# A fused attention and maxout kernel: one low part, one sum, one minimum and two weight loads change place

## The chip, the cores and the metric

The kernel runs on one core of one Trainium2 chip. Its engines are TensorE (PE in the profile; PEld is its weight load), VectorE (DVE), ScalarE (ACT), GpSimd (POOL) and SyncE (SP), which here issues all the transfers. The metric is the time on the device in microseconds, as the median of several runs.

## The reference

Two steps, all in fp32. First, an attention through 32 inducing points: for each of 4 batches of 12,544 tokens with 128 channels, the inducing points attend over the tokens and give 32 states `h`, and then each token attends over these 32 states. Second, each token of the result goes through a maxout layer.

```python
def mab(q, kv):
    s = scale * (q @ kv.transpose(0, 2, 1))
    s = s - s.max(-1, keepdims=True)
    a = np.exp(s)
    a /= a.sum(-1, keepdims=True) + 1e-09
    return a @ kv
h = mab(I, x)
x = mab(x, h)                                       # B 4, N 12544, m 32, C 128
h = np.maximum(np.maximum(x @ w1, x @ w2), x @ w3)  # 128 by 768 each
out = h @ w_out                                     # 768 by 128
```

The weights of the maxout layer arrive as 64-bit numbers and are turned into fp32 on the chip.

## The kernel before

**Tiling.** The tokens of a batch are 98 tiles of 128, in seven groups: group 0 has 2 tiles, the others 16. For the second step a group of 16 tiles is four chunks of 512 tokens (the small group is one chunk of 256), so a batch has 25 chunks, and 768 hidden columns are six blocks of 128. One chunk with one block is a *slot*; there are 600.

**The products of a slot.** Since the maximum of three is max(x·w1 − x·w2, x·w3 − x·w2, 0) + x·w2, and x is the softmax's weights times the 32 states, the states are first multiplied by the weights (`us`, in a high and a low part), and each slot takes them by the weights `pT` of a chunk (again high and low parts, stacked on 128 partitions). A slot has these pieces, in `advance` (a step `s` handles the slots around `s`) and `stage2`:

- PE: `pu` (L663) of slot s+1, then `pv` (L669) of slot s, each into one of two banks;
- ScalarE: `ru = relu(pu)` (L678), then `hi`, the high part of `h` of the slot before (L685);
- VectorE: `h = max(pv, ru)` (L696);
- GpSimd, or for listed slots VectorE: `lo = h - hi` (L693 and L699). `LOWVEC = (23, 0, 15, 18)`, and `LOWLAST` in the last batch, list the slots of a group of 24 whose low part VectorE takes; it is then issued one step later, behind the next `h`;
- PE, six slots later (`LAG`): three products into the chunk's sum, `hi` by the high part of `w_out` (L719), `hi` by its low part (L720), `lo` by the high part (L721); once for a chunk L718 adds the part x·w2·w_out.

`h` has five buffers, `hi` and `lo` ten by name, of which the tile framework's own choice leaves fewer. A step's next `pv` writes the bank that `h` two slots back must have read.

**What runs between.** While batch b goes through its slots, the attention of batch b+1 is done group by group: products (L282), the greatest score and its spread to all quadrants (`attend_max` L292, `attend_column` L299, `attend_spread` L306), the running least value of its negative `mneg` (`attend_least`, L310 and L313), weights (L321), transposes (L335), sums over tokens (L345), and the addition to the running states, `hs` and `lst`, with the factor `al` (`attend_scale` L364, `attend_add` L382). The softmax of the second step runs one group ahead (`scores_steps`, L595 to L628). A plan by slot number says at which step each piece is issued; the engines run their instructions in that order.

**Before the main loop.** Batch 0's attention comes first, in `phase1_first`: loads of x by group, transposes on PE (L272), the same steps as above, and between them the conversion of the four weights in the steps of `WORK` ("2t" is step t, L171, of the weight of index 2, which is w1; index 3 is w3, 0 is w2, 1 is `w_out`). `LOADS` is the order in which SyncE issues the first loads: 0 to 6 are groups of x, 7 to 10 the weights w2, `w_out`, w1, w3. A group of 16 tiles has five buffers (`XB`), so that group 6 waits for the buffer of group 1.

Then `ORDER` is a list written out by hand, from about 42 to 54 us: `a` and `b` are the next step of the softmax of group 0 and of group 1; `0` to `3` a high part of `us` and `c` its low part; `m` another product for `us`; `p` and `q` the rows `pT` of chunk 0 and of chunk 1 (PE transposes and a copy for the first, L640 and L645; four DMAs for the second, L648); `d` two products of the identity that nobody reads (`keep_busy`, L393); `s` a step of `advance`; `S` the scores of group 2.

## Time and profile before

| | us |
|---|---|
| median of 3 runs | 832.28 |
| the runs | 831.1, 832.28, 832.58 |
| the profiled execution | 830.93 |
| its span, from the first to the last instruction | 828.8 |

| engine | busy, us | share of the span |
|---|---|---|
| TensorE products | 813.8 | 98% |
| TensorE weight loads | 632.9 | 76% |
| ScalarE | 743.5 | 90% |
| VectorE | 644.0 | 78% |
| GpSimd | 646.7 | 78% |

A share is an average over the span. What a stretch is bound by is read from the chain of waits and from the timeline, in which each row gives the start, the duration, the engine, the line with its operation, output and inputs, and in brackets how long the engine was idle before and whose work ended that. Products are pipelined on TensorE, so rows overlap, and the distance of two starts says more than a duration.

### The profile page before, as it was taken

How to read it: one execution, taken by the hardware profiler on the slowest of the kernel's cores; microseconds unless marked ns; L12 is line 12 of the kernel's file. 1: busy time of each engine (PE TensorE's matmuls, PEld its weight loads, DVE VectorE, ACT ScalarE, POOL GpSimd, SP SyncE). 2: the span in 40 equal slices, each digit the busy share in tenths (PEclk: the TensorE clock that was granted, in tenths of full speed). 3: DMA queues.
4: the chain of work that ended last, by engine and by line, in shares of the span. 5: the costliest groups of instructions: out<-in, count | busy, mean ns of one | idle time of the engine just before them, and what ended most of it. 6: DMA issues, size and time to landing. Idle time of an engine off the chain costs nothing.

```text
span 828.8 us, 14799 instructions
## 1 busy us (share of the span) xinstructions
PE 813.8 (98%) x4608; PEld 632.9 (76%) x4608; DVE 644.0 (78%) x1109; ACT 743.5 (90%) x1542; POOL 646.7 (78%) x517
## 2 busy tenths in 40 slices
PE   7989999999999999999999999999999999999998
PEld 5657778777787787777777777877778778778786
DVE  4878778878787688787787877877878778877864
ACT  6679889898898898898999989989889899999996
POOL 1368779778798697787887877877879888888887
PEclk9999999999999999999999999999999999999999
DMA  9744534433443445244334362441233222222221
GB/s 342 288 149 124 199 85 159 163 118 106 133 139 120 143 156 167 80 161 158 112 106 134 114 210 77 153 128 52 64 82 88 71 77 77 64 77 72 70 77 52
DMA packets 44062, 102.51 MB, mean 124 GB/s; under 512 B 9552, under 2 KB 13264, under 8 KB 38736
## 3 DMA queue, kind: packets, MB, share of 16 engines
q1 hardware_dynamic: 43984, 101.57, 37.8%
q8 instruction: 37, 0.61, 0.3%
q14 instruction: 41, 0.34, 0.1%
HBM read 48.12 MB, written 25.69 MB: 89 GB/s over the span
## 4 chain that ended last, share of the span: by engine, by line
PE 94%; DMA 2%; DVE 1%; SPq 1%; issue 1%; ACT 0%; DVEq 0%; ACTq 0%
PE acc L719 17%; PE acc L720 16%; PE acc L721 16%; PE pv L669 16%; PE pu L663 16%; PE aux L582 3%; PE acc L718 3%; PE acc L345 3%; PE aux L282 2%; DMA xg<-in_x_dram 2%; SPq L100 1%; DVE h L696 0%; PE acc L306 0%; PE acc L525 0%; SPq L120 0%
## 5 line engine op out<-in xcount | busy, mean ns | idle before, releaser
L693 POOL TENSOR_TENSOR lo<-h,hi 128x512 fp32r<-128x512 f32 (+1 forms) x498 | 631.5, 1296 | 141.5 <-ACT hi L685 102.9
L696 DVE TENSOR_TENSOR h<-pv,ru 128x512 f32<-128x512 f32 (+1 forms) x600 | 402.9, 675 | 152.3 <-PE pv L669 72.5
L678 ACT ACTIVATE ru<-pu 128x512 f32<-128x512 f32 (+1 forms) x600 | 375.4, 626 | 54.6 <-PE pu L663 50.6
L685 ACT CAST hi<-h 128x512 fp32r<-128x512 f32 (+1 forms) x600 | 386.5, 644 | 7.2 <-DVE h L696 6.8
L719 PE MATMUL acc<-hi,wo_hi 128*128 128x512 f32 (+1 forms) x600 | 237.2, 395 | 0.0
L669 PE MATMUL pv<-pT,us 128*128 128x512 f32 (+1 forms) x600 | 232.8, 388 | 3.8 <-DVE h L696 3.2
L663 PE MATMUL pu<-pT,us 128*128 128x512 f32 (+1 forms) x600 | 232.7, 388 | 0.3 <-DMA pT<-pl 0.3
L720 PE MATMUL acc<-hi,wo_lo 128*128 128x512 f32 (+1 forms) x600 | 231.6, 386 | 0.0
L721 PE MATMUL acc<-lo,wo_hi 128*128 128x512 f32 (+1 forms) x600 | 231.3, 385 | 0.0
L719 PEld LDWEIGHTS acc<-hi,wo_hi 128*128 128x128 f32 x600 | 112.7, 188 | 31.8 <-issue 10.4
L669 PEld LDWEIGHTS pv<-pT,us 128*128 128x128 f32 x600 | 112.6, 188 | 30.6 <-DVE h L696 8.8
L663 PEld LDWEIGHTS pu<-pT,us 128*128 128x128 f32 x600 | 112.6, 188 | 26.2 <-ACT ru L678 2.5
L721 PEld LDWEIGHTS acc<-lo,wo_hi 128*128 128x128 f32 x600 | 112.7, 188 | 23.1
L720 PEld LDWEIGHTS acc<-hi,wo_lo 128*128 128x128 f32 x600 | 112.8, 188 | 21.1
L699 DVE TENSOR_TENSOR lo<-h,hi 128x512 fp32r<-128x512 f32 x102 | 76.6, 751 | 6.4 <-PE acc L721 3.6
L726 ACT COPY o<-acc 128x512 f32<-128x512 f32 (+1 forms) x100 | 61.4, 614 | 3.0 <-PE acc L721 3.0
L718 PE MATMUL acc<-pT,us 128*128 128x512 f32 (+1 forms) x100 | 38.8, 388 | 0.0
L345 PEld LDWEIGHTS acc<-xg,aT 128*32 128x32 f32 x768 | 21.1, 110 | 11.4 <-issue 7.2
L282 PE MATMUL aux<-xT,iT 128*32 128x512 f32 x192 | 25.3, 598 | 1.6 <-ACT xT L274 1.6
L345 PE MATMUL acc<-xg,aT 128*32 128x128 f32 x768 | 25.6, 274 | 0.0
L582 PE MATMUL aux<-xT,hT 128*32 128x512 f32 x192 | 25.5, 604 | 0.0
L192 POOL TENSOR_TENSOR rest<-rest,t 128x768 f32<-128x768 f32 x3 | 5.5, 1826 | 23.3 <-DVE rest L184 23.3
(115 smaller groups left out, 451.8 us busy)
## 6 DMA issues: line engine op xcount, KB each, us to landing
out_dram<-o SPq DMA_DIRECT2D x96, 256.0 KB, 2.0
xg<-in_x_dram SPq DMA_DIRECT2D x23, 1024.0 KB, 6.6
xT<-in_xt_dram SPq DMA_DIRECT2D x18, 1024.0 KB, 5.2
pT<-ph SPq DMA_DIRECT2D x192, 64.0 KB, 2.0
pT<-pl SPq DMA_DIRECT2D x192, 64.0 KB, 2.0
raw<-in_w_dram SPq DMA_DIRECT2D x3, 768.0 KB, 14.9
us<-uh SPq DMA_DIRECT2D x24, 52.0 KB, 1.9
us<-ul SPq DMA_DIRECT2D x24, 52.0 KB, 1.9
```

The lines of the kernel that those rows point to most:

```text
L345: nc.tensor.matmul(out=hps[q * M : (q + 1) * M, :C], lhsT=aT[:, t * M : (t + 1) * M], rhs=xg[:, t, :], start=(t < NQ), stop=(t + NQ >= nt),)
L663: nc.tensor.matmul(out=pu[:, :w], lhsT=state[c.b]["us"][:, 2 * j * P : (2 * j + 1) * P], rhs=c.pT[:, :w], start=True, stop=True)
L669: nc.tensor.matmul(out=pv[:, : d.w], lhsT=state[d.b]["us"][:, (2 * j + 1) * P : (2 * j + 2) * P], rhs=d.pT[:, : d.w], start=True, stop=True,)
L678: nc.scalar.activation(out=ru[:, :w], in_=pu[:, :w], func=AF.Relu)
L685: nc.scalar.copy(out=hi[:, : c.w], in_=h[:, : c.w])
L693: nc.gpsimd.tensor_sub(**args)
L696: nc.vector.tensor_max(out=h[:, : d.w], in0=pv[:, : d.w], in1=relus.pop(s)[:, : d.w])
L699: nc.vector.tensor_sub(**low)
L718: nc.tensor.matmul(out=c.acc[:, :w], lhsT=us[:, 2 * DF :], rhs=c.pT[:, :w], start=True, stop=False)
L719: nc.tensor.matmul(out=c.acc[:, :w], lhsT=wo_hi[:, j, :], rhs=c.hh[j][:, :w], start=False, stop=False)
L720: nc.tensor.matmul(out=c.acc[:, :w], lhsT=wo_lo[:, j, :], rhs=c.hh[j][:, :w], start=False, stop=False)
L721: nc.tensor.matmul(out=c.acc[:, :w], lhsT=wo_hi[:, j, :], rhs=c.hl[j][:, :w], start=False, stop=(j == NJ - 1))
```

## The change

Six edits.

1. `LOADS`: group 5 of x is loaded before w1, and group 6 before w3.
2. `ORDER`: of the steps of the softmax of group 1, two come earlier; the scores of group 2 (`S`) and the last product for `us` (`m`) come behind them; one of five pairs of idle products (`d`) is gone.
3. In the softmax of the first two groups of batch 0, the sum with 1e-9 is an instruction of VectorE instead of ScalarE.
4. `attend_least`: the least value of a group goes to a free column of the PSUM bank, and the minimum with the value before reads it there.
5. `attend_add`: the running sum of weights `lst` is updated by ScalarE (scale `al`, bias the new sum) instead of VectorE.
6. `Chunk.low`: the low part of slot 0 of group 1 goes to GpSimd, in each batch.

```diff
-    LOADS = (0, 1, 2, 7, 3, 8, 4, 9, 5, 10, 6)
+    LOADS = (0, 1, 2, 7, 3, 8, 4, 5, 9, 6, 10)
...
-    ORDER = "a a a a b a a b 0 c d m b a a b a b p d b 1 c s S m b b b s b q 2 c d s 3 c s d s s d s"
+    ORDER = "a a a a b a a b 0 c d m b a b a b a p d b 1 c s b b b s S m b q 2 c s 3 c s d s s d s"
...
-        nc.vector.tensor_reduce(out=st["mneg"][:, gi : gi + 1], in_=st["mp"][:, :NQ], axis=AX.X, op=ALU.min)
-        if b > 0 and gi > 0:
-
-            nc.vector.tensor_tensor(
-                out=st["mneg"][:, gi : gi + 1], in0=st["mneg"][:, gi : gi + 1], in1=st["mneg"][:, gi - 1 : gi], op=ALU.min
-            )
+        new, mp = st["mneg"][:, gi : gi + 1], st["mp"]
+        if b == 0 or gi == 0:
+            nc.vector.tensor_reduce(out=new, in_=mp[:, :NQ], axis=AX.X, op=ALU.min)
+        else:
+
+            nc.vector.tensor_reduce(out=mp[:, NQ : NQ + 1], in_=mp[:, :NQ], axis=AX.X, op=ALU.min)
+            nc.vector.tensor_tensor(out=new, in0=mp[:, NQ : NQ + 1], in1=st["mneg"][:, gi - 1 : gi], op=ALU.min)
...
-        for total, new in ((st["hs"], st["h"][:, :C]), (st["l1"], st["lst"][:, gi : gi + 1])):
-            nc.vector.scalar_tensor_tensor(
-                out=total, in0=total, scalar=st["al"], in1=new, op0=ALU.mult, op1=ALU.add
-            )
+        nc.vector.scalar_tensor_tensor(
+            out=st["hs"], in0=st["hs"], scalar=st["al"], in1=st["h"][:, :C], op0=ALU.mult, op1=ALU.add
+        )
+        nc.scalar.activation(
+            out=st["l1"], in_=st["l1"], func=AF.Identity, scale=st["al"], bias=st["lst"][:, gi : gi + 1]
+        )
...
-        nc.scalar.activation(out=rs[:, :nt], in_=rs[:, :nt], func=AF.Identity, bias=eps)
+        if b == 0 and gi < 2:
+            nc.vector.tensor_scalar_add(out=rs[:, :nt], in0=rs[:, :nt], scalar1=1e-9)
+        else:
+            nc.scalar.activation(out=rs[:, :nt], in_=rs[:, :nt], func=AF.Identity, bias=eps)
...
-            return self.q is not None and NJ * self.q + k in (LOWVEC if self.b + 1 < B else LOWLAST)
+            if self.q is None or (self.gi == 1 and self.q == k == 0):
+                return False
+            return NJ * self.q + k in (LOWVEC if self.b + 1 < B else LOWLAST)
```

SyncE's queue, early loads, before (`xg` is a group of x, `raw` a weight):

```order
L100 DMA xg_128<-in_x_dram 128x2048
L120 DMA raw_130<-in_w1_dram 128x1536
L100 DMA xg_132<-in_x_dram 128x2048
L120 DMA raw_134<-in_w3_dram 128x1536
L100 DMA xg_136<-in_x_dram 128x2048
L100 DMA xgs_138<-in_x_dram 128x256
```

and in the changed kernel:

```order
L100 DMA xg_128<-in_x_dram 128x2048
L100 DMA xg_130<-in_x_dram 128x2048
L120 DMA raw_132<-in_w1_dram 128x1536
L100 DMA xg_134<-in_x_dram 128x2048
L120 DMA raw_136<-in_w3_dram 128x1536
L100 DMA xgs_138<-in_x_dram 128x256
```

Groups 5 and 6 each pass one weight; w3 stands behind group 6.

VectorE where the slots of 512 columns of batch 0 begin, before (`pv` is the bank that `h` reads, `aux` the scores of the next group):

```order
L696 TENSOR_TENSOR h_733<-pv0_83,ru_712 128x512
L696 TENSOR_TENSOR h_746<-pv1_84,ru_727 128x512
L696 TENSOR_TENSOR h_761<-pv0_83,ru_741 128x512
L699 TENSOR_TENSOR lo_745<-h_733,hi_743 128x512
L696 TENSOR_TENSOR h_779<-pv1_84,ru_755 128x512
L595 STREAM_TRANSPOSE aux0_79<-aux0_79 128x512
L696 TENSOR_TENSOR h_793<-pv0_83,ru_773 128x512
```

and in the changed kernel:

```order
L702 TENSOR_TENSOR h_731<-pv0_83,ru_710 128x512
L702 TENSOR_TENSOR h_745<-pv1_84,ru_725 128x512
L702 TENSOR_TENSOR h_760<-pv0_83,ru_739 128x512
L702 TENSOR_TENSOR h_777<-pv1_84,ru_754 128x512
L598 STREAM_TRANSPOSE aux0_79<-aux0_79 128x512
L702 TENSOR_TENSOR h_791<-pv0_83,ru_771 128x512
```

The low part of slot 0 no longer stands between the third and the fourth `h`; it is on GpSimd, first in a row of 15 low parts of 512 columns where there were 14.

VectorE where the states of the next batch are added up, one of 18 such places, before:

```order
L595 STREAM_TRANSPOSE aux_79<-aux_79 128x512
L382 SCALAR_TENSOR_TENSOR hs<-hs,al,acc_86 128x128
L382 SCALAR_TENSOR_TENSOR lst<-lst,al 128x1
L696 TENSOR_TENSOR h<-pv_83,ru 128x512
L292 TENSOR_REDUCE mq<-aux_80 128x1
```

and ScalarE at the same place in the changed kernel:

```order
L684 ACTIVATE ru<-pu_81 128x512
L691 CAST hi<-h 128x512
L385 ACTIVATE lst<-lst,al 128x1
L684 ACTIVATE ru<-pu_82 128x512
L691 CAST hi<-h 128x512
```

On VectorE `h` now follows the addition to `hs` directly; on ScalarE the addition to `lst` stands between a high part and the next `ru`.

## Rows read from the trace of the kernel before

**Rows 1.** The page: busy us (share) xinstructions by engine; granted clock in 40 slices.

```profile
PE 813.8 (98%) x4608; PEld 632.9 (76%) x4608; DVE 644.0 (78%) x1109; ACT 743.5 (90%) x1542; POOL 646.7 (78%) x517
...
PEclk9999999999999999999999999999999999999999
```

**Rows 2.** Chain of waits, 0 to 70 us: start us, us, what.

```profile
9.11 15.24 DMA xg<-in_x_dram
...
63.26 0.23 PE acc L721
```

**Rows 3.** Timeline 18 to 31 us: start, us, engine, line, work, [idle before <-releaser].

```profile
22.54 1.07 PE L282 MATMUL aux<-xT,iT 128*32 128x512 f32 x8
...
23.85 0.54 DVE L171 TENSOR_SCALAR t<-raw 128x768 uint32<-128x768 uint32 x1
...
24.39 1.09 PE L272 MATMUL pu<-ident,xg 128*128 128x128 f32 x8 [0.78 <-DMA xg<-in_x_dram]
...
27.72 0.16 DVE L310 TENSOR_REDUCE mneg<-acc 128x1 f32<-128x4 f32 x1 [0.68 <-PE acc L306]
```

**Rows 4.** Timeline 44 to 55 us, all engines.

```profile
45.46 1.26 POOL L541 TENSOR_TENSOR us<-uf,us 64x512 fp32r<-64x512 f32 x1 [1.93 <-issue]
...
46.77 0.37 ACT L645 CAST pT<-pu 128x256 fp32r<-128x256 f32 x1 [0.29 <-PE pu L640]
...
49.41 0.58 ACT L625 CAST ph<-aux 128x512 fp32r<-128x512 f32 x1 [0.40 <-DVE aux L622]
...
50.03 1.22 SPq L648 DMA_DIRECT2D pT<-ph  x2
...
53.99 0.50 PE L663 MATMUL pu<-pT,us 128*128 128x512 f32 x1 [0.34 <-DMA pT<-pl]
```

**Rows 5.** Timeline 58.4 to 62.2 us, batch 0, start of group 1.

```profile
58.56 1.64 DVE L699 TENSOR_TENSOR lo<-h,hi 128x512 fp32r<-128x512 f32 x1 [0.90 <-PE acc L721]
...
59.12 0.40 PE L663 MATMUL pu<-pT,us 128*128 128x512 f32 x1
...
60.12 0.68 DVE L696 TENSOR_TENSOR h<-pv,ru 128x512 f32<-128x512 f32 x1
...
60.86 0.50 PE L669 MATMUL pv<-pT,us 128*128 128x512 f32 x1 [1.34 <-DVE h L696]
...
61.55 0.39 PE L663 MATMUL pu<-pT,us 128*128 128x512 f32 x1
...
62.07 0.50 PE L669 MATMUL pv<-pT,us 128*128 128x512 f32 x1
```

**Rows 6.** Timeline of TensorE, same place in batch 1 and in batch 3.

```profile
257.42 0.40 PE L663 MATMUL pu<-pT,us 128*128 128x512 f32 x1
258.28 0.50 PE L669 MATMUL pv<-pT,us 128*128 128x512 f32 x1 [0.47 <-DVE h L696]
...
652.23 0.40 PE L663 MATMUL pu<-pT,us 128*128 128x512 f32 x1
653.22 0.50 PE L669 MATMUL pv<-pT,us 128*128 128x512 f32 x1 [0.59 <-DVE h L696]
```

**Rows 7.** Busy time by engine in a stretch: PE, PEld, DVE, ACT, POOL, clock, DMA, GB/s.

```profile
60.00:75.50 15.50, 14.51 (x71) 11.00 (x72) 13.27 (x25) 14.22 (x31) 15.17 (x12) 1.00 0.43 147
```

**Rows 8.** L382, L313: ns min/median/max; timeline of ScalarE and TensorE, 192 to 204.

```profile
L382 DVE SCALAR_TENSOR_TENSOR lst<-lst,al x18: 213/735/742, 93.8 to 602.1; 128x1 f32<-128x1 f32 x18
...
L313 DVE TENSOR_TENSOR mneg<-mneg x18: 159/454/502, 84.3 to 592.9; 128x1 f32<-128x1 f32 x18
...
192.10 0.62 ACT L685 CAST hi<-h 128x512 fp32r<-128x512 f32 x1 [0.28 <-DVE h L696]
...
200.66 0.35 ACT L364 ACTIVATE al<-mneg 128x1 f32<-128x1 f32 x1
...
202.66 0.39 PE L721 MATMUL acc<-lo,wo_hi 128*128 128x512 f32 x1
...
203.04 0.50 PE L663 MATMUL pu<-pT,us 128*128 128x512 f32 x1
```

## The prediction

> **What bounds the kernel now.** I read the busy times first: PE is busy for 813.8 of 828.8 us, 98%, and its granted clock stands at full level (9 in every slice) [rows 1]. The chain of waits agrees: 94% of it is PE. Its steps in the main loop are 0.23 us each, start to start, for a product of 128x512 [rows 2]. So an edit is worth something in two cases alone: if it starts the main loop earlier, or if it closes a gap in PE's row of starts. I then looked for these gaps in the timeline of PE: every place where two starts lie further apart than 0.23 us (0.12 us for the products of 256 columns of a batch's first chunk).
>
> Before the main loop the chain stands on the loads of x: one step of 15.24 us ends at 24.39 [rows 2], where PE begins the transposes of group 5, 0.78 us after it ran dry [rows 3]. Between 44 and 54 us the softmax of groups 0 and 1 leads to two sets of products, and PE's last wait there is 0.34 us for the rows of `pT` at 53.99 [rows 4].
>
> In the main loop, after 55 us, I found two kinds of gaps and no third. The first is at the start of group 1 in each batch. In batch 0 `pu` starts at 59.12 and `pv` only at 60.86; then `pu` at 61.55 and `pv` at 62.07 [rows 5]. Less the regular 0.23 that is 1.51 and 0.29 us. Behind each gap the next product starts 0.34 instead of 0.23 us later, 0.11 more: 2.02 us together. Batch 1 has 0.86 between the same two, so 0.63, and batch 3 has 0.99, so 0.76 [rows 6]; batch 2 is as batch 1; each has a second gap of 0.30, and both restarts of 0.11. That is 1.15 + 1.15 + 1.28. All four: 5.6 us. The second kind is small: in batches 0 to 2 `pu` starts twice 0.38 us after the product before it, at 203.04 for one [rows 8], and loses 0.15 and the restart of 0.11; six times 0.26 is 1.6 us.
>
> **The change part by part.** *The loads.* Transfers follow each other without a gap there, so moving w1 behind group 5 gives group 5 its place: about the 2.5 us earlier that w1 takes, near 21.9. Then PE needn't wait at 24.39: the products at 22.54 end at 23.61 [rows 3], and group 5 can follow at about 23.6. That is 0.8 us. What is late next: w1 itself. It lands where group 5 landed, near 24.35, and VectorE's `t` of w1, which ran at 23.85, must wait till then, 0.5 us [rows 3]. VectorE carries that through `mq`, `aT` and two passes over w1 to the least value at 27.72, ahead of which it idled 0.68 [rows 3]: absorbed there, but the `mq` behind comes 0.6 rather than 0.8 earlier. w3 comes one group of x later, some 2.5 us, still ahead of its first step on VectorE, which has the work of group 5 before it. SyncE now holds w3 behind group 6's load, which waits for a buffer of x; only small loads are queued behind. I take 0.7; the ends are 0.3 (all of the wait for w1 passed on) and 1.0.
>
> *The order behind `h`.* The exponential of group 1 and its sums go ahead of group 0's last steps, so `pT` of chunk 0, copied at 46.77 [rows 4], comes some 0.75 later. But the wait of PE at 53.99 is for chunk 1, and its path goes through `ph` at 49.41 and four DMAs from 50.03 [rows 4]. On ScalarE the queue ahead of `ph` (pT, us, uf, ru) adds up to the same within 0.1 us. I take 0.1 of gain. If the late `pT` passed on, it would cost up to 0.75 less the wait of 0.34 that it can fill, 0.4; if `ph` comes as early as its inputs, it gives 0.5. The sum with 1e-9 on VectorE takes the place of an instruction on ScalarE and two handovers, and is in these numbers. GpSimd works at 45.46 for 1.26 us [rows 4]. In the new order this piece begins a little earlier and ends before the sum of 128x16 is due.
>
> The Trainium skill ("SBUF — State Buffer", Who interferes with whom) says that a VectorE operation that goes from SBUF to SBUF in its two-port mode shuts out a GpSimd operation, and the other way round, for the whole instruction. That speaks against this move: the sum would wait up to the 1.26 us of that row if GpSimd were still at work, and the forecast would be 0.9 us later at most (an estimate by that page); with GpSimd idle by then it changes nothing, and no row here shows the case.
>
> *The low part.* At the first gap `pv` waits for `h`, and `h` waits on VectorE behind the low part of slot 0: 58.56, 1.64 us long [rows 5]. It started late because its buffer is released by a product (L721) that had only then run. The change gives it to GpSimd, where it takes its turn in the buffers one step sooner, so that the release it needs is an earlier one. VectorE can then take that `h` as soon as its product has ended, in place of the low part at 58.56, and finish by about 59.2, where before it began at 60.12 [rows 5]; `pv` is due at 59.35. The price is one more low part on GpSimd: 15.17 us for 12 is 1.26 each [rows 7]. GpSimd then has 15 in a row, 19 us. PE's work in these slots is some 16.5 us: six of 2 x 0.23 + 3 x 0.12 beside the chunk of 256, nine of 5 x 0.23, and about 1.2 of attention. So GpSimd falls back by 2.5 us, two slots, over the stretch; it starts with a lead of about four slots (five buffers of `h`, and the product that reads a low part runs six slots behind). Following its queue by hand from 55 us, each `h` is held back by at most 0.3 us, and `pv` has 0.3 to 0.7 of slack. So the first gap closes in all batches, and of the second I leave 0.1 and a restart in each of three batches: 5.6 less 0.65 is 4.95 us.
>
> *The sum of weights.* VectorE's 128x1 addition has a median of 735 ns, at best 213 [rows 8]; eighteen times. In the block that ends in the small gaps it holds `h` back, and ScalarE's cast of `hi` at 192.10 waits 0.28 for that `h` [rows 8]. From there ScalarE runs without idle time to 203, where `pu` waits for its `ru`. On ScalarE the addition costs at most the 0.35 of `al`, its neighbour of the same shape [rows 8], and it stands ahead of the block, where ScalarE still idles. VectorE is 0.7 lighter there, the wait of 0.28 goes, and the block ends about 0.3 earlier, where 0.15 is wanted. I take all 1.6; the other end is a loss of 0.35 in each of the six blocks, 2.1, if ScalarE has no idle time to spend and the wait stays.
>
> *The running minimum* reads PSUM in place of SBUF: 159 ns at best, 454 in the median now [rows 8]. VectorE gains up to 0.3 us eighteen times, none of it before a gap of PE. The bank is read 0.2 later, by a product with 0.7 of slack. Nothing.
>
> The sum: 0.7 + 0.1 + 4.95 + 1.6 = 7.35 us. The profiled run took 830.93, so 823.6, with a span near 821.4. The median of the runs shown is 832.28, 1.35 above the profiled one; with the same distance the median comes to **824.9**.
>
> **The rivals.** *ScalarE's gaps stay*: the block is so tight that a later ru is late all the same. For it: ScalarE is busy 90% [rows 1]. Against it: 0.3 is gained where 0.15 is missing. Then 826.5. *GpSimd takes over*: its 15 low parts hold `h` back instead of VectorE's one. For it: GpSimd was busy 15.17 of 15.5 us there [rows 7], so it has no room to catch up. A stretch that it paces would start earlier by the gap and end later by 1.26, so it keeps 2.02 less 1.26 in batch 0 and nothing in the others: 0.8 of 4.95, so 829.1; half of it, 827.4. Against it: the lead of four slots at the start. *The clock falls*, and this one ends slower than before: one of five pairs of idle products that fill PE's pauses between 44 and 55 us is gone, PE drops from 2.4 to 1.2 GHz and stays there until its steady work at 62. Each us of PE's work at the lower level then costs one more; with about 10 us of it between 50 and 62 the kernel loses 10 and gains 7.35: 834.9. It decides once more than 7.35 us of work run at the lower level. Against it: PE paused 1.34 us ahead of 60.86 [rows 5] and the clock stayed at 9 [rows 1].
>
> The Trainium skill ("TensorE: Matmul & The Clock Gate", The HAM clock gate) says that the clock falls back to 1.2 GHz after an idle time; by that rule a pause that the pair covered could set it off, and the time would be that of this rival. The trace has no fall after any pause, so it bears the rule out nowhere.
>
> **How the numbers follow.** The forecast as a whole has 0.67; ScalarE's gaps staying 0.15; GpSimd taking half or more 0.12; the clock 0.04; two of the losses together, near 831, 0.02. The range takes the ends of the small terms below (0.3 more from the loads, 0.4 from the order, the 0.65 left at the second gaps, and the runs' own spread of 0.7 us), of which some three quarters at once: 823.3. Above it reaches over ScalarE's gaps and the half of GpSimd's, with 0.5 for the order: 827.9. About 0.2%, 1.7 us, is what a measurement of this kernel can tell from no change: faster by more has 0.92, within it 0.04, slower 0.04.
>
> **What would show it.** Right: `pu` to `pv` at the start of group 1 at 0.23 us in all batches; transposes of group 5 at 23.6 and the first `pu` of chunk 1 near 53.2; no `pu` that waits for `ru` near 203; PE's busy share up by 0.6 points or more. Wrong: GpSimd as releaser of `h` in the 15 slots behind; a clock below 9 in the third slice; `t` of w1 that moves the products behind 27.7; an `h` that still waits for a low part elsewhere. Most of the forecast hangs on the low part: if its 4.95 fall away, the rest gives 829.9.

## The result, and the profile after

The changed kernel takes 823.61 us in the median of four runs (823.18 to 824.16); with the runs of the kernel before beside it the ratio is 0.9898, with an interval of 0.9884 to 0.9911. So it is faster, by some 8 us. The forecast of 824.9 was 0.9911 of 832.28, at the very edge of that interval: the gain was a little larger than forecast, and the terms it consists of are other ones.

The profiled execution took 823.18 us with a span of 821.3, where the forecast had 823.6 and 821.4. These are the lines of its page that answer to [rows 1]: busy us (share) xinstructions, the granted clock in 40 slices, and the chain of waits by engine.

```profile
PE 809.3 (99%) x4604; PEld 633.3 (77%) x4604; DVE 626.7 (76%) x1089; ACT 743.2 (90%) x1558; POOL 650.5 (79%) x521
...
PEclk9999999999999999999999999999999999999999
...
PE 95%; DMA 2%; DVE 1%; SPq 1%; ACT 1%; issue 0%; ACTq 0%; DVEq 0%
```

PE's share went from 98.2% to 98.5%, 0.36 points up where the prediction's signs asked for 0.6: only 3.0 of the 7.6 us that the span lost were idle time by the profile, which counts a product as busy until its modelled end. VectorE has 17 us less to do: 18 sums of weights and four low parts are gone, and the minimum is shorter. ScalarE got 16 instructions more, the 18 additions less two sums with 1e-9, and is no busier.

To see where the time went I split the span at two products: the first transpose of group 5 of x, at 24.39 before [rows 3], and the first `pu` of chunk 1, at 53.99 before [rows 4]. The chain of waits after, 0 to 70 us (start us, us, what), has the same places (the transposes of group 5 start at 24.08 in the timeline of PE, without a wait), and the last product in the timeline is the other end:

```profile
19.86 1.09 PE pu L272 x8
...
24.15 1.02 PE pu L272 x8
...
53.48 0.50 PE pu L669
```

```profile
817.15 0.39 PE L729 MATMUL acc<-lo,wo_hi 128*128 128x512 f32 x1
```

From the first `pu` of chunk 1 to the end of the last product it was 771.1 us before (53.99 to 825.11) and is 764.1 after: 7.0 of the 7.5 us lie in the main loop, and 0.5 ahead of it. I call these 771.1 and 764.1 the *main time* from here on. It has little of the spread of whole runs, which comes from the loads ahead of it (below), but it is read from one trace of each kernel. Two traces whose edits lie ahead of it altogether, b_loads and b_order, have 771.4 and 771.1, and five traces of the changed main loop lie at 763.9 to 764.1: a difference of 0.3 is not told from nothing.

Every gap that the prediction listed is gone. Two of its signs at the start came out later than forecast, group 5 at 24.08 for 23.6 and the first `pu` of chunk 1 at 53.48 for 53.2. The timeline of PE after, start of group 1 in batch 0, against [rows 5]:

```profile
59.42 0.41 PE L669 MATMUL pu<-pT,us 128*128 128x512 f32 x1
...
59.68 0.50 PE L675 MATMUL pv<-pT,us 128*128 128x512 f32 x1
60.02 0.40 PE L726 MATMUL acc<-pT,us 128*128 128x512 f32 x1
```

From `pu` to `pv` it is 0.26 us where it was 1.74. The restart behind it is still there, 0.34 us to the next product, at this place in all four batches. Of the 14 gaps over 0.12 us that stood in the main loop, none is left. One new one has come, in the last batch, where `pu` at 655.94 is followed by `pv` at 656.35, 0.18 too late. It belongs to the low part: of the traces below, the eleven with that low part on GpSimd have 0.12 to 0.18 there, and of the seven others only b_low_now has a gap near this place, the 1.86 us below. GpSimd meanwhile is full in the stretch of [rows 7], by the windows (us, PE, PEld, DVE, ACT, POOL busy, clock, DMA share, GB/s):

```profile
59.50:75.00 15.50, 15.50 (x76) 11.83 (x76) 12.30 (x24) 15.25 (x35) 15.50 (x13) 1.00 0.45 151
```

15.50 of 15.50 us on GpSimd, and 15.50 of 15.50 on PE: GpSimd takes back nothing, as the forecast had it. So far everything reads as if the prediction were right. What the parts are worth, however, only the runs below tell.

### The profile page after: what moved, and what is told of

Read it like the earlier page. It is cut to its first block, busy times and chain, and to the rows that moved or that the text cites. A ratio compares the mean times of both kernels' runs of the same rounds, so it can differ in the third digit from the quotient of the medians.

```text
span 821.3 us, 14724 instructions
## 1 busy us (share of the span) xinstructions
PE 809.3 (99%) x4604; PEld 633.3 (77%) x4604; DVE 626.7 (76%) x1089; ACT 743.2 (90%) x1558; POOL 650.5 (79%) x521
## 4 chain that ended last, share of the span: by engine, by line
PE 95%; DMA 2%; DVE 1%; SPq 1%; ACT 1%; issue 0%; ACTq 0%; DVEq 0%
PE acc L727 17%; PE pv L675 16%; PE acc L728 16%; PE acc L729 16%; PE pu L669 16%; PE aux L585 3%; PE acc L726 3%; PE acc L346 3%; PE aux L282 2%; DMA xg<-in_x_dram 2%; PE acc L306 0%; PE pu L272 0%; SPq L100 0%; PE pv L272 0%; PE aux L551 0%; DMA pT<-pl 0%
## 5 line engine op out<-in xcount | busy, mean ns | idle before, releaser
L727 PEld LDWEIGHTS acc<-hi,wo_hi 128*128 128x128 f32 x600 | 112.7, 188 | 31.7 <-issue 10.4
L705 DVE TENSOR_TENSOR lo<-h,hi 128x512 fp32r<-128x512 f32 x98 | 71.1, 725 | 0.7 <-ACT hi L691 0.7
```

The costliest lines, as they stand in the source:

```text
L705: nc.vector.tensor_sub(**low)
L727: nc.tensor.matmul(out=c.acc[:, :w], lhsT=wo_hi[:, j, :], rhs=c.hh[j][:, :w], start=False, stop=False)
```

## The experiments

The main time of each run stands behind its measurement, since it tells parts of a microsecond apart. Runs named b_ are the kernel before with something added, a_ the changed kernel with something undone or added.

### The low part alone (b_low)

```diff
-            return self.q is not None and NJ * self.q + k in (LOWVEC if self.b + 1 < B else LOWLAST)
+            if self.q is None or (self.gi == 1 and self.q == k == 0):
+                return False
+            return NJ * self.q + k in (LOWVEC if self.b + 1 < B else LOWLAST)
```

> The kernel before with the low part of slot 0 of group 1 on GpSimd, and nothing else. Theory (the gaps at the start of group 1 come from VectorE's late low part): pu to pv there comes down from 1.74, 0.86, 0.86 and 0.99 us to at most 0.3, the gaps near 169 and 203 stay, and the span falls by 4.8 to 5.2 us, to 823.6 to 824.0. Rival (GpSimd's 15 low parts in a row hold h back): 0.8 to 2.5 us of gain, with h waiting for GpSimd in the 15 slots.

Measured: 827.64 us, ratio 0.9951 (0.9934 to 0.9969), span 824.9, main time 767.2, 3.95 less than before. That is less than the 4.8 to 5.2 expected and more than the rival's 2.5. The gaps at the start of group 1 are gone. Of the six small ones five stay; in the block of the sixth `pv` waits 0.5 us from 556.5 on instead, which the next experiment explains. GpSimd as a new bound is refuted.

### The sum of weights alone (b_lst)

```diff
-        for total, new in ((st["hs"], st["h"][:, :C]), (st["l1"], st["lst"][:, gi : gi + 1])):
-            nc.vector.scalar_tensor_tensor(
-                out=total, in0=total, scalar=st["al"], in1=new, op0=ALU.mult, op1=ALU.add
-            )
+        nc.vector.scalar_tensor_tensor(
+            out=st["hs"], in0=st["hs"], scalar=st["al"], in1=st["h"][:, :C], op0=ALU.mult, op1=ALU.add
+        )
+        nc.scalar.activation(
+            out=st["l1"], in_=st["l1"], func=AF.Identity, scale=st["al"], bias=st["lst"][:, gi : gi + 1]
+        )
```

> The kernel before with the sum of weights on ScalarE, and nothing else. Theory (VectorE's long 128x1 addition starts the row of late work that ends in the six small gaps): pu no longer waits for ru near 169 and 203 and their like, the span falls by 1.6 us, 2.2 at most, to 826.6 to 827.2, and the gaps at the start of group 1 stay. Rival (ScalarE is full in that block and an addition more makes it later): the six gaps stay or grow by up to 0.35 each, span 828.8 to 830.9.

Measured: 832.57 us, ratio 0.9997 (0.9981 to 1.0013), span 829.0, main time 770.7: 0.4 us less, not 1.6. My theory falls, and so does the rival's reason. `pu` no longer waits near 169 and 203, as expected, but six gaps of about the same size, 0.2 us, have come 3.5 us earlier, and in them `pv` waits for `h`. The timeline of PE, of VectorE and of GpSimd there:

```profile
165.59 0.39 PE L665 MATMUL pu<-pT,us 128*128 128x512 f32 x1
166.02 0.50 PE L671 MATMUL pv<-pT,us 128*128 128x512 f32 x1
```

```profile
164.15 0.15 DVE L310 TENSOR_REDUCE mneg<-acc 128x1 f32<-128x4 f32 x1
164.34 1.03 DVE L313 TENSOR_TENSOR mneg<-mneg 128x1 f32<-128x1 f32 x1
165.29 1.27 DVE L698 TENSOR_TENSOR h<-pv,ru 128x512 f32<-128x512 f32 x2
```

```profile
161.54 5.06 POOL L695 TENSOR_TENSOR lo<-h,hi 128x512 fp32r<-128x512 f32 x4
```

The minimum of two columns, L313, takes 1.03 us for 128x1 elements, and `h` stands behind it. In the profile before it took 454 ns in the median and 502 at most [rows 8], and 159 or 160 in these six blocks. By the starts and ends of the single instructions in the trace, it now starts 0.28 us behind the start of GpSimd's third low part and ends 0.02 us behind its end; each of the 18 minima of b_lst ends 0.01 to 0.02 us behind the low part that ran when it started. In the six blocks before it started 0.06 us ahead of the end of one. So VectorE and GpSimd are shifted against each other, and the minimum now hits a low part at its start and sits out nearly all of it. The prediction had given the edit that cures this "nothing". The same instruction is behind the new gap of b_low, by VectorE's and PE's timelines there:

```profile
555.62 0.98 DVE L313 TENSOR_TENSOR mneg<-mneg 128x1 f32<-128x1 f32 x1
556.53 1.28 DVE L696 TENSOR_TENSOR h<-pv,ru 128x512 f32<-128x512 f32 x2
```

```profile
556.53 0.39 PE L663 MATMUL pu<-pT,us 128*128 128x512 f32 x1
557.26 0.50 PE L669 MATMUL pv<-pT,us 128*128 128x512 f32 x1 [0.34 <-DVE h L696]
```

### Both small sums (b_sums), and each of them undone (a_mneg, a_lstdve)

b_sums is the kernel before with the diff of b_lst and the new `attend_least` (the running minimum reads PSUM). a_mneg and a_lstdve are the changed kernel with one of the two put back:

```diff
 # a_mneg
...
-            nc.vector.tensor_reduce(out=mp[:, NQ : NQ + 1], in_=mp[:, :NQ], axis=AX.X, op=ALU.min)
-            nc.vector.tensor_tensor(out=new, in0=mp[:, NQ : NQ + 1], in1=st["mneg"][:, gi - 1 : gi], op=ALU.min)
+            nc.vector.tensor_tensor(
+                out=st["mneg"][:, gi : gi + 1], in0=st["mneg"][:, gi : gi + 1], in1=st["mneg"][:, gi - 1 : gi], op=ALU.min
+            )
...
 # a_lstdve
...
-        nc.scalar.activation(
-            out=st["l1"], in_=st["l1"], func=AF.Identity, scale=st["al"], bias=st["lst"][:, gi : gi + 1]
-        )
+            nc.vector.scalar_tensor_tensor(
+                out=total, in0=total, scalar=st["al"], in1=new, op0=ALU.mult, op1=ALU.add
+            )
...
```

> The kernel before with edits 4 and 5 together, the running minimum from PSUM and the sum of weights on ScalarE. Edit 5 alone moved the six gaps by 3 us and gave 0.4 us from the first pu of chunk 1 to the end (771.11 before). Theory (the two hide each other): no pu or pv waits near 166, 169, 200 and 203 and their like, and the time falls by 1.6 to 2.7 us. Rival (other work of VectorE or ScalarE keeps them): it falls by 0.4 to 0.8.

Measured: 828.98 us, ratio 0.9972 (0.9955 to 0.9989), span 826.7, main time 768.7: 2.4 us less, where edit 5 alone gave 0.4. No gap is left but those at the start of group 1.

> The changed kernel with the running minimum read from SBUF again (edit 4 undone). The prediction gave this edit nothing. Theory (the 128x1 minimum with two inputs in SBUF waits for GpSimd's low part, 1.0 us at worst, and holds h back): gaps of 0.2 us or more between pu and pv, with h as releaser, come back about 3 us before the places near 169 and 203 and their like, and the time from the first pu of chunk 1 to the end grows from 764.06 by 1.5 to 2.7 us. Rival (the edit is worth nothing, and the sum of weights alone closes the six gaps): 764.06 within 0.3.

Measured: 825.06 us in two runs, span 823.0, main time 766.0, 1.9 more than the changed kernel. Six gaps of 0.2 us are back, as in b_lst:

```profile
161.12 1.03 DVE L313 TENSOR_TENSOR mneg<-mneg 128x1 f32<-128x1 f32 x1
162.07 1.27 DVE L701 TENSOR_TENSOR h<-pv,ru 128x512 f32<-128x512 f32 x2
```

```profile
162.38 0.39 PE L668 MATMUL pu<-pT,us 128*128 128x512 f32 x1
162.80 0.50 PE L674 MATMUL pv<-pT,us 128*128 128x512 f32 x1
```

> The changed kernel with the sum of weights on VectorE again (edit 5 undone). Theory (both 128x1 additions are needed to close the six gaps, since each alone is enough to hold h back): the gaps between the last product of a slot and pu come back, 0.15 and a restart of 0.11 at six places, 1.6 us, up to 2.3. Rival (the minimum was the whole cause, and ScalarE's addition costs as much as it gives): within 0.3 us of 764.06 from the first pu of chunk 1 to the end.

Measured: 827.41 us in three runs, span 825.5, main time 766.3, 2.2 more. The six gaps of [rows 8] are back at their old place, ahead of `pu`:

```profile
167.64 0.40 PE L727 MATMUL acc<-lo,wo_hi 128*128 128x512 f32 x1
168.00 0.50 PE L667 MATMUL pu<-pT,us 128*128 128x512 f32 x1
```

So the two edits belong together. On the kernel before, the sum alone gives 0.4 us and both give 2.4; the minimum alone wasn't run there. With the low part moved as well the main time goes from 767.2 (b_low) to 766.3 with the minimum alone (a_lstdve), to 766.0 with the sum alone (a_mneg) and to 764.1 with both: 0.9, 1.2 and 3.1 us. The pair gives 1.0 us more than its parts there, because either instruction is enough to push the same block over its limit. The line of the minimum in the changed kernel, by its source line (ns min/median/max), shows what reading PSUM does; the row of before is in [rows 8]:

```profile
L316 DVE TENSOR_TENSOR mneg<-acc,mneg x18: 157/158/160, 81.9 to 586.4; 128x1 f32<-128x1 f32 x18
```

and in b_lst, with both inputs in SBUF:

```profile
L313 DVE TENSOR_TENSOR mneg<-mneg x18: 261/467/1032, 84.8 to 593.0; 128x1 f32<-128x1 f32 x18
```

158 ns eighteen times, whatever GpSimd does, against 261 to 1032. The Trainium skill ("SBUF — State Buffer", Who interferes with whom) says that a VectorE instruction with two SBUF inputs contends with a GpSimd instruction that reads SBUF, and calls the contention an exclusive lock. The trace agrees: 1.03 us here against GpSimd's 1.26 for a low part [rows 7], and the wait is gone once one input comes from PSUM. By this page of the Trainium skill the sum of weights and the low parts of VectorE are of the same kind.

### Has ScalarE room for the addition? (a_lst3)

```diff
+        for _ in range(2):
+            nc.scalar.activation(
+                out=wk.tile([P, 1], F32, name="spare", tag="spare"), in_=st["l1"], func=AF.Identity,
+                scale=st["al"], bias=st["lst"][:, gi : gi + 1],
+            )
```

> The changed kernel with two more additions of the same shape on ScalarE behind each of the 18 sums of weights; nobody reads them. Theory (ScalarE has idle time at these places): their 0.2 to 0.35 us each are absorbed and the span grows by less than 0.5 us. Rival (ScalarE is at its limit there and the change only just fits): the six gaps near 169 and 203 come back, 0.26 each or more, and the span grows by 1.6 us or more, up to 36 times 0.35, 12 us.

Measured: 829.0 us in two runs, span 827.0, main time 768.9, 4.8 more than the changed kernel. The rival is right: `pu` waits again at six places, by PE's timeline at the first of them:

```profile
167.65 0.40 PE L734 MATMUL acc<-lo,wo_hi 128*128 128x512 f32 x1
168.12 0.50 PE L674 MATMUL pu<-pT,us 128*128 128x512 f32 x1
```

0.47 us from start to start, 0.24 too much; further small waits make up the rest. It is 36 additions and 4.8 us, 0.13 each on average, of the 0.28 to 0.29 from the start of such an addition to the start of the next instruction of ScalarE: a little under half of their cost comes through. The prediction placed the one addition "ahead of the block, where ScalarE still idles". The idle time there is enough for one addition, not for three.

### Why VectorE's low part was late (b_low_now, b_low_late)

The prediction's reason was the buffer: issued one step late, the low part gets a buffer that a later product releases. The first kernel leaves it on VectorE but issues it at once; the second gives it to GpSimd, but one step late.

```diff
 # b_low_now
-            if c.low(j):
+            if c.low(j) and c.gi == 1 and c.q == j == 0:
+                nc.vector.tensor_sub(**args)
+            elif c.low(j):
                 pipe["low"] = args
 # b_low_late
+        first = pipe.pop("first", False)
...
                 pipe["low"] = args
+                pipe["first"] = c.gi == 1 and c.q == j == 0
...
-            nc.vector.tensor_sub(**low)
+            (nc.gpsimd if first else nc.vector).tensor_sub(**low)
```

> The kernel before, with slot 0's low part still on VectorE but issued at once, ahead of the next h, so that it takes its buffer in turn. Theory (what makes it late is the release of its buffer, not VectorE): it starts about when hi is there, near 57.3 in place of 58.56, the first gap of batch 0 falls from 1.51 to 0.3 or less and the span by 4 us or more. Rival (VectorE has too much to do there, or its low part is slow beside GpSimd's): the gaps keep half or more of their 5.6 us.

Measured: 830.07 us in two runs, ratio 0.997 (0.9941 to 0.9999), span 827.9, main time 769.8: 1.3 us less. The gaps in batches 1 and 2 are gone, so there it is enough to issue it at once, with an earlier release; in the last batch 0.2 of its gap is left. In batch 0 a gap of 0.97 stays. VectorE and PE at that place:

```profile
57.73 0.69 DVE L691 TENSOR_TENSOR lo<-h,hi 128x512 fp32r<-128x512 f32 x1 [1.35 <-ACT hi L685]
58.34 2.03 DVE L698 TENSOR_TENSOR h<-pv,ru 128x512 f32<-128x512 f32 x3
```

```profile
57.88 0.40 PE L663 MATMUL pu<-pT,us 128*128 128x512 f32 x1
59.08 0.50 PE L669 MATMUL pv<-pT,us 128*128 128x512 f32 x1 [0.81 <-DVE h L698]
```

The low part starts at once when its input `hi` is there and takes 0.69 us, not 1.64; but now VectorE waits 1.35 us for `hi`, with `h` behind it. And in the last batch a gap of 1.86 us has opened at 660.9, behind another low part of VectorE of 1.41 us. So my theory falls, and of the rival the number comes out but not the reason: the release is one cause; another is that VectorE, in its order, has `h` standing behind any low part that waits for anything.

The length is a third, which the prediction passed over. The 1.64 us of [rows 5] are 0.95 more than the 0.69 here, and in the kernel before GpSimd was at work beside it:

```profile
58.36 2.96 POOL L693 TENSOR_TENSOR lo<-h,hi 128x512 fp32r<-128x512 f32 x2 [1.27 <-PE acc L720]
```

The first of these two takes 1.29 us, to 59.65, and VectorE's low part from 58.56 ends 0.55 behind that: by these times the wait of the minimum above, at a larger instruction, though no run has it alone. In the other batches it took 1.59 to 1.70.

> The kernel before, with slot 0's low part on GpSimd but issued one step late, as VectorE's was, so that it takes a later buffer. Theory (the release of the buffer is what counts): GpSimd waits till about 58.4 for L721 with all its later low parts queued behind it, loses about 1.3 us in a row of 15 that has no room to catch up, and the first gap stays, or one of like size opens some slots later: the span falls by less than 3 us. Rival (it is enough that VectorE is rid of it): the span falls by about 5 us.

Measured: 827.16 us in two runs, ratio 0.9935 (0.9906 to 0.9964), span 825.2, main time 767.0: 4.1 us less, as much as b_low. The rival is right in kind, if not at its 5 us. On GpSimd the late buffer costs next to nothing; beside the gap in the last batch, one of 0.4 us at 78.8 is all:

```profile
58.83 1.31 POOL L695 TENSOR_TENSOR lo<-h,hi 128x512 fp32r<-128x512 f32 x1 [1.27 <-PE acc L722]
60.09 1.30 POOL L701 TENSOR_TENSOR lo<-h,hi 128x512 fp32r<-128x512 f32 x1
```

GpSimd waits here for a product as it did before, with the low part of the next slot (L695), and slot 0's (L701) stands right behind it; but only low parts are queued there, and PE reads them six slots later.

### The low part undone in the changed kernel (a_lowdve)

```diff
-            if self.q is None or (self.gi == 1 and self.q == k == 0):
-                return False
-            return NJ * self.q + k in (LOWVEC if self.b + 1 < B else LOWLAST)
+            return self.q is not None and NJ * self.q + k in (LOWVEC if self.b + 1 < B else LOWLAST)
```

> The changed kernel with the low part of slot 0 of group 1 on VectorE again (edit 6 undone). Theory (its gain stands alone): the gaps of 1.5 and 0.64 to 0.76 us at the start of group 1 come back with the small ones behind, and the time from the first pu of chunk 1 to the end grows from 764.06 by 4.0 to 5.1 us. Rival (part of the gain needs the other edits or is theirs): by less than 3.5.

Measured: 829.64 us, span 829.2 in the profiled run, main time 768.8, 4.7 us more than the changed kernel. The gaps are back at 1.51, 0.65, 0.65 and 0.76 us, with the small ones of 0.28 to 0.29 behind. Its gain stands alone.

### The loads alone (b_loads) and the order alone (b_order)

```diff
 # b_loads
-    LOADS = (0, 1, 2, 7, 3, 8, 4, 9, 5, 10, 6)
+    LOADS = (0, 1, 2, 7, 3, 8, 4, 5, 9, 6, 10)
 # b_order, with the sum with 1e-9 of the first two groups on VectorE
-    ORDER = "a a a a b a a b 0 c d m b a a b a b p d b 1 c s S m b b b s b q 2 c d s 3 c s d s s d s"
+    ORDER = "a a a a b a a b 0 c d m b a b a b a p d b 1 c s b b b s S m b q 2 c s 3 c s d s s d s"
```

> The kernel before with the new order of loads, and nothing else. The trace of the changed kernel has group 2 and group 4 of x land 0.54 us later than before, and only 0.3 of the 0.7 us forecast is left at the first state of batch 0. Theory A (the order itself does that: a group of x in place of a weight in the queue takes bandwidth from the groups ahead of it): group 2 lands near 10.75 again and hT starts 0.3 us earlier than before. Theory B (the start of the loads differs from run to run): group 2 lands near 10.2 and hT starts 0.7 to 0.9 us earlier.

Measured: 831.25 us, ratio 0.9991 (0.9981 to 1.0001). In its profiled run (span 831.4) group 5 begins only at 26.66, 2.3 us later than before. Neither theory holds as it stood; the windows of this run show a third thing (us, PE, PEld, DVE, ACT, POOL busy, clock, DMA share, GB/s):

```profile
18.00:20.00 2.00, 0.81 (x8) 0.00 (x0) 1.90 (x4) 1.19 (x2) 0.00 (x0) 1.00 0.99 401
20.00:22.00 2.00, 1.16 (x10) 1.17 (x11) 2.00 (x4) 0.75 (x3) 1.52 (x1) 0.95 1.00 416
22.00:24.00 2.00, 2.00 (x17) 1.63 (x18) 1.99 (x2) 1.71 (x5) 0.30 (x1) 0.50 0.26 107
24.00:26.00 2.00, 2.00 (x36) 1.42 (x30) 0.23 (x2) 0.53 (x2) 0.00 (x0) 0.70 0.02 6
```

PE waits for group 4, which comes at 20.8 here, and is busy 1.97 of 4 us; then the granted clock falls to 0.5, and the second half of group 4's transposes (1.87 us for 1.04) and the sums behind them (1.85 for 1.08) take nearly twice as long. At group 5 it is back. That is the rival of the falling clock, at a place where I hadn't looked for it. The runs on this are below.

> The kernel before with the new hand-written order and the sum with 1e-9 on VectorE, and nothing else. Theory (chunk 1's rows come a little earlier): from the first state to the first pu of chunk 1 it takes 12.27 us, as in the changed kernel, in place of 12.48; the span falls by 0.2 us. Rival (the later pT of chunk 0 is passed on): 0.4 us more. Group 2 of x lands where it lands before, near 10.2, if the order of loads sets that, and anywhere from 10.2 to 10.8 if runs differ.

Measured: 831.23 us, ratio 0.9993 (0.9982 to 1.0003); main time 771.1, as before. Counted from the start of group 5 to the first `pu` of chunk 1 it takes 29.41 us; the changed kernel and the five traces of it with another edit undone or added have 29.40 to 29.47, and the kernel before and its variants with the old order 29.56 to 29.63 (b_lst 29.77). So the order gives 0.2 us, and the later `pT` of chunk 0 costs nothing. Group 2 began at 11.6 here with the old order of loads: runs differ in that by themselves.

### The idle products (a_nobusy)

The changed kernel with the four pairs left out that remain in its list:

```diff
-    ORDER = "a a a a b a a b 0 c d m b a b a b a p d b 1 c s b b b s S m b q 2 c s 3 c s d s s d s"
+    ORDER = "a a a a b a a b 0 c m b a b a b a p b 1 c s b b b s S m b q 2 c s 3 c s s s s"
```

> The changed kernel with all pairs of idle products between 44 and 55 us left out, where the change left out one of five. If the pairs keep the clock up (the rival of the prediction that ends slower): the granted clock falls below 9 in the third slice of 40 or behind it, and each us of work at the lower level adds one. If they don't matter here: the clock stays at 9 and the span is within 0.3 us of 821.3, or up to 0.5 shorter.

Measured: 824.47 us in two runs (825.73 for the profiled one, 823.2 for the other, which is as fast as the changed kernel), span 823.9, main time 765.5, 1.4 more than the changed kernel. The slices of the page show 9 everywhere, because a slice averages 20 us; the windows show the fall (us, PE, PEld, DVE, ACT, POOL busy, clock, DMA share, GB/s):

```profile
47.00:50.00 3.00, 1.89 (x14) 0.80 (x13) 2.65 (x6) 1.87 (x5) 0.73 (x2) 1.00 0.36 153
50.00:54.70 4.70, 2.86 (x18) 1.51 (x10) 3.71 (x8) 4.17 (x13) 3.37 (x5) 1.00 0.27 67
54.70:58.00 3.30, 3.25 (x10) 2.81 (x11) 1.12 (x2) 1.86 (x5) 2.14 (x3) 0.52 0.59 119
58.00:62.00 4.00, 4.00 (x31) 3.25 (x30) 2.90 (x5) 3.84 (x8) 3.00 (x3) 0.97 0.92 340
```

and those of the changed kernel:

```profile
47.00:50.00 3.00, 2.54 (x19) 1.32 (x17) 2.40 (x5) 2.81 (x7) 1.29 (x1) 1.00 0.01 3
50.00:53.50 3.50, 2.74 (x18) 2.13 (x17) 2.80 (x7) 2.98 (x10) 2.20 (x4) 1.00 0.37 91
53.50:57.00 3.50, 3.50 (x27) 2.82 (x28) 2.35 (x4) 2.92 (x7) 2.28 (x4) 1.00 0.48 92
```

Without the pairs PE is busy 1.89 of 3.00 and 2.86 of 4.70 us, and then runs at 0.52 of full speed, the level of 1.2 GHz, for 3.3 us, until it has worked without a pause. With four of five pairs it is busy 2.54 of 3.00 and 2.74 of 3.50, and the clock stays. So the rival of the falling clock names a real mechanism, which the change stays clear of in its profiled run. Its price was put too high: 1.4 us in this one trace, not 10, for the clock came back by 58 us. The Trainium skill ("TensorE: Matmul & The Clock Gate", The HAM clock gate) has the clock fall to 1.2 GHz after idle time and rise with sustained work. The trace agrees in that the clock is at 0.52 behind a stretch with pauses and back at 0.97 in work without them; PE was not idle as a whole ahead of the fall.

### The clock during the loads (a_again, a_loads, a_busy, a_busy1)

a_again is the changed kernel once more; a_loads has the old `LOADS` in it; the other two have idle products where PE waits for the loads:

```diff
 # a_busy; a_busy1 has 1 in place of 4
                 if k == 0:
                     start_group(0, gi)
+                    if 1 < gi < NG - 2:
+                        keep_busy(4, bank_u[0])
```

> The changed kernel itself, as the measure for the two runs beside it. The spread of a kernel's times goes with its granted clock so far: of 41 times of the kernel before, the 28 with a mean clock of 0.999 or more lie at 830.9 to 832.7 us, the 13 below at 832.8 to 836.2. If the clock's falls while TensorE waits for the early loads make that spread, the changed kernel shows it too: most times at 823.2 to 824.2 with a clock of 0.999 or more, and one in three or so at 825 to 828 with less.

> The changed kernel with the old order of loads (edit 1 undone). Theory (the order gives 0.3 to 0.7 us where the clock holds, and doesn't change how often it falls): the times with a clock of 0.999 or more lie 0.3 to 0.7 above those of the changed kernel beside it. Rival (the order is worth nothing): within 0.2 of them. A third, that the new order makes TensorE wait longer at groups 4 and 5 and so lets the clock fall more often: fewer times with a low clock here than for the changed kernel.

> The changed kernel with four idle products of 128x128 ahead of the transposes of groups 2, 3 and 4 of x, where TensorE waits for the loads. Theory (the clock falls there because TensorE idles, and this makes the slow third of the times): the clock stays at 0.999 or more in all times, all lie within 1 us of the fastest, and the mean of the times falls by about 0.7 us while the fastest stays. Rival (the falls come from elsewhere, or four products are too few): times with a clock below 0.999 as often as in the changed kernel beside it.

> The changed kernel with one idle product of 128x128 ahead of the transposes of groups 2, 3 and 4 of x. Four took 1.0 us at each place, where TensorE waits 0.35 to 0.7, and cost 1.6 us in the median, with the clock at 0.999 or more in all six times. Theory (one product of 0.25 us lies within the wait): the times with a full clock are those of the changed kernel, 823.2 to 823.8, and a clock below 0.999 is rarer than the one in four so far. Rival (one is too little, or delays the transposes all the same): as many low clocks, or 0.2 us and more on the median.

Measured, with the 66 times of the kernel before that stand beside the runs: 43 have a mean clock of 0.999 or more and lie at 830.9 to 832.7 (median 831.52), 23 have less and lie at 832.1 to 836.2. So the spread of the times is for the most part the clock.

- a_again: 823.4 to 823.8 in five times, median 823.69, none with a low clock. The third of low clocks that I expected didn't come in five.
- a_loads: 824.02, five times with a full clock from 823.15 to 824.51, median 823.80, and one of 826.64 with 0.998. Where the clock holds the old order is 0.1 us behind a_again; b_loads, the other way round, has 831.24 in nine such times, 0.3 ahead of the kernel before. So by the medians the new order is worth 0.1 to 0.3 us, which the spread of these times, 1.4 and 1.5 us, does not tell from nothing. The run of 826.64 is the profiled one: here too group 4 came late (21.58), PE was busy 0.42 of the 2 us before 22, and the clock stood at 0.50 in the next two. The old order lets it fall as well. Over all runs the clock was below 0.999 in 33 of 108 times with the old order and in 8 of 34 with the new one (without the runs with other idle products): no difference can be seen.
- a_busy: 825.31, 1.6 us more than a_again, six times with a full clock. The four products take 1.0 us at each place, by PE's timeline, where the wait is 0.35 to 0.7:

```profile
20.20 1.16 PE L396 MATMUL pu<-ident 128*128 128x128 f32 x8
21.20 1.04 PE L272 MATMUL pu<-ident,xg 128*128 128x128 f32 x8
```

- a_busy1: 824.98, with a low clock in two of six times; the fastest is 824.13. So one product doesn't rule the fall out, and still costs some 0.6 us.

None of these is better than the changed kernel. That PE's waiting for loads comes ahead of the clock's fall is in the rows of the traces that have it; that idle products prevent it is not shown: at 8 low clocks in 34 times, six full ones in a row, as in a_busy, come by chance one time in five. What makes group 4 late in some runs is open.

## Why the prediction was right, and where it was wrong

The time came out close, 823.61 for 824.9; the sum behind it did so in part by luck. Three steps failed. *The running minimum* was put at nothing, and is worth 1.9 us in the changed kernel. *The sum of weights* was given the whole 1.6, and alone is worth 0.4. And "the same distance" from the profiled run to the median, 1.35, was 0.43. Step by step, in main time where that is what a step moves:

| step | forecast, us | measured, us | by |
|---|---|---|---|
| the loads | 0.7 | 0.1 to 0.3 where the clock holds | b_loads, a_loads |
| the order | 0.1 | 0.2 | b_order |
| the low part | 4.95 | 4.0 alone, 4.7 in the changed kernel | b_low, a_lowdve |
| sum of weights | 1.6 | 0.4 alone, 2.2 undone in the changed kernel | b_lst, a_lstdve |
| running minimum | 0 | 1.9 undone in the changed kernel | a_mneg |
| both small sums | 1.6 | 2.4 | b_sums |
| profiled run to median | 1.35 | 0.43 | the result |

**What bounds it**: right. The main loop's gain is gaps of PE's starts that closed, and above 0.12 us the list of gaps was complete; some 0.7 us came from smaller ones.

**The low part**: the size was right, 4.7 of 4.95. The difference is the new gap of 0.18 in the last batch with its restart; of the listed gaps about as much was left, the four restarts, as the forecast had left. The reason given was part of it. The release of the buffer delayed VectorE, but b_low_late has the same late buffer and all the gain of b_low; what counts is whether `h` stands behind the instruction that waits. And 0.95 of the low part's 1.64 us was, by the times, a wait for GpSimd, which the prediction read as its length. The hand-made walk through GpSimd's queue held: a window of 15.50 us with GpSimd never idle and PE without a gap.

**The two small sums**: here the prediction failed, in the step *The running minimum*: "none of it before a gap of PE. Nothing." I looked for the gaps that the minimum causes in the trace before, and there it causes none: in the six blocks it takes 159 or 160 ns, since it meets GpSimd at the end of a low part. With the sum of weights gone from VectorE it meets GpSimd at the start of one, takes 1.02 to 1.03 us, and makes six gaps of about the same size. The step *The sum of weights* failed for the same reason from the other side: it took the wait that was visible for the only one and gave the edit all 1.6 us, where alone it gives 0.4. The two errors cancelled for the most part, which is luck: the prediction's sum for both is 1.6, and 2.4 was measured. Most of the 0.8 more are waits far below 0.1 us, many of them, that I had not counted as gaps: behind products of 512 columns, starts that lie up to 0.04 us over the regular distance of 0.227 add up to 3.6 us before, and to 2.9 in b_sums.

**The loads**: the step was sized from one trace. The transposes of group 2 begin at 10.2 us in it and at 10.4 to 12.5 in the others, with either order, so its group 5 was among the earliest as well (24.4; 24.4 to 25.2 in the others with the old order and a full clock). The wait ahead of group 5 did go, as forecast. But from group 2 to group 5, where the clock holds and no idle products are added, it takes 13.3 us in the four traces with the new order and 13.4 to 14.2 in the seven with the old, and the 14.2 is the trace that the 0.8 was read from. Nor does w1 take 2.5 us: its 768 KB at the 416 GB/s of 18 to 24 us are 1.9, while 2.5 is what a group of x takes; since PE was the bound at 23.6, that changed nothing. Measured are 0.1 to 0.3 in whole times; in the profiled run the chain is 0.3 earlier at 31 us. The bound below, 0.3, should have been nothing.

**The order.** The wait for GpSimd that was weighed against the sum with 1e-9 did not come: that sum takes 0.16 us at 46.61, and GpSimd's piece had ended at 46.41.

**From the profiled run to the median**: the distance of 1.35 us that I added was no property of the kernel. Over the 43 times with a full clock the median of the kernel before is 831.52, 0.59 above the profiled run; the changed kernel's median lies 0.43 above its own. The clock of the three runs shown is not on record, so what made their 1.35 stays open. This distance is 0.9 of the 1.3 us by which the median came out below the forecast. The other 0.4 is in the profiled runs, which differ by 7.75 where 7.35 was forecast: 0.5 more in the main loop, since the 0.8 more from the small sums is partly taken up by the low part, 0.3 less ahead of it, and 0.2 outside the span (2.1 us before, 1.9 after).

**The rivals**: ScalarE's gaps did go, but not by the edit that I gave them to. ScalarE has room for the one addition and not for three (a_lst3). GpSimd didn't take over. The clock does fall, more often than the chance I gave it, but at the loads, ahead of the place that the change touches, and before and after the change alike; at the place named it fell with all five pairs gone and held with one gone; what lies between was not run. The sentence that the trace has no fall after any pause overlooks its end, where the clock is at 0.5 from 828.1 us on, after PE's last product has ended at 825.11.

## What to carry to other kernels

A wait that isn't there in the trace may come with the edit that removes another: when two instructions in the same block can both hold the critical one back, an edit alone can measure far below its worth with the other, and only the pair shows it (0.4 and 2.4 us here). Give a small VectorE instruction an input in PSUM where GpSimd streams from SBUF beside it; its best and its worst time in the line's row (159 to 502 ns, 157 to 160) tell whether it suffers. On an engine that works in order, ask of an instruction that may wait who stands behind it: the same low part, one step late, cost 4 us on VectorE and nothing that could be seen on GpSimd.

## What the runs showed of the hardware that was not expected

- A minimum of 128x1 elements with both inputs in SBUF took from 0.16 to 1.03 us on VectorE, by where it fell against GpSimd's low parts of 1.26 us, and in b_lst it ended 0.01 to 0.02 us behind the low part under way each time; with one input in PSUM it took 0.16 each time.
- An addition of 128x1 on ScalarE, 0.38 us long, added 0.13 us to the whole, 36 times, in a kernel where ScalarE is busy 90% of the span.
- In 5 of 18 traces PE's clock fell to half for 2 to 4 us during the first 26 us, behind waits for the early loads; the mean clock of such a run is 0.995 to 0.998, and its time up to 4.6 us longer. The same loads bring group 2 at 10.2 to 12.5 us in different runs. A comparison by stretches, from a product to a product, is good to some 0.3 us in spite of it.
- Without idle products PE's clock was at 0.52 for 3.3 us in the one trace of that kernel, which cost 1.4 us; the page's 40 slices of 20 us don't show it.
